# Weights' decoding without a clamp, the normalisation's scaling on ScalarE, and other places for banks, weight sums and scales at the passage to the second network

## Chip, cores and metric

The kernel runs on one core of one Trainium2 chip. The metric is the device time of one execution in microseconds (us); the time of the kernel before is the median of three runs. One further execution was profiled, and all rows below are of that one. The core has a matrix engine (TensorE, PE in the rows; its weight loads are PEld), and VectorE (DVE), ScalarE (ACT), GpSimd (POOL) and SyncE (SP), which here only issues transfers. Each of them works through its own queue in order. Matmuls write into PSUM, which has eight banks of 128 x 512 words.

## Reference

Three stages follow each other: an attention through 32 packed vectors per head, a first network with a softmax-weighted activation and a normalisation (moe), and a second network with a maximum over three products (moe2).

```python
p_packed = sm_attn(p, k, v)                    # 8 images, 8 heads, 576 x 64
x = sm_attn(q, p_packed, p_packed)             # laid out as 4608 x 512
h = x @ w_in                                   # 4608 x 1024
solu = h * softmax(h)
ln = (solu - mean(solu)) / sqrt(var(solu) + 1e-06) * g_ln
y = ln @ w_out                                 # 4608 x 512
h2 = maximum(maximum(y @ w1, y @ w2), y @ w3)  # 4608 x 768
out = h2 @ w_out2                              # 4608 x 512
```

The weights come as 64-bit floating point numbers, and the kernel turns them into 32-bit ones itself. `sums`, `squares` and `powers` hold one number per token and tile, from which the factor `z` of each token's row is worked out; it is applied when the rows of the result are stored.

## The kernel before

The **first phase** covers attention and moe in 36 tiles of 128 tokens. For each tile `tok_hidden` makes h on TensorE (two PSUM banks of `ps_h`, one buffer), the row maximum on VectorE (L506), the exponential on ScalarE (L508), the product with h on VectorE (L510), the negative mean `nmu` (L512), the squares on ScalarE (L513), two small operations on a power of two (L517, L521), and the scaled row u = (u + nmu) * pw on VectorE (L524). The rows of four tiles are transposed on TensorE (L557), split into a high and a low part by ScalarE (`lh`, L563) and VectorE (`ll`, L564), and multiplied by the weights into y (L575): sixteen steps, eight for each half of the output columns. Each half has two banks, `y0` and `y1` of `ps_y`, which are copied out as `yt` by ScalarE (L242) and VectorE (L244) and stored to `ydram`.

An image's attention is prepared by `Packed` in steps that fill gaps between tiles. `values` scales the packed result into `ppz` (L379, two operations of VectorE), TensorE transposes it (L383) and VectorE copies it out as `ppT` (L244). `product` then multiplies `ppT` by `w_in_sb` (L395).

**Decoding.** `decode` turns a piece of 64-bit weights in `raw` into 32-bit ones: ScalarE takes the high word's absolute value into `dt` (L116), VectorE clamps it (L121), shifts and masks it (L122), puts the sign back (L125), isolates the power (L128) and multiplies the low word by it, into `dt` again (L130); GpSimd adds both parts (L135). `dt` of the later pieces has one buffer. Eight pieces of 512 columns for `w_in` and four for `w_out` are followed by 56 of 256 columns for the rest of `w_out` and for moe2, whose results go to `wdram` and `wodram`. The letter strings in `CFG` place these steps in the tiles: each `D` finishes one piece and begins the next, `A` issues its start early, `T` a transposition, `y` a step of y, `F` a step of an image's preparation.

**The passage.** After the last tile the steps of the last y group alternate with the list `before`: sums and splits of y for moe2 (`sums_y`, L680; `splits_y`, L695 and L696), and the weight sums of moe2's first cell (`split_w`: splits L623 and L624, sums L630). Then come the operations of `scales` on VectorE (L531 to L549) and **moe2** in 54 cells, each of seven products into four banks m0 to m3 (L719), added up on VectorE as `u` (L754), `v` (L758), `kept`, `cur` and `r`. The weight sums of cell n + 1 are chores of cell n.

A scheduler orders all of this: it takes instructions in the order of the code, as priorities, and places each engine's queue by its own estimates and by the buffers that are free. The order on an engine can so differ from that of the code.

Of the kernel before, what the change touches and what calls it, by code (L numbers as in the profile page):

```python
# [8 lines left out]
F32 = mybir.dt.float32  # L9
# [9 lines left out]
def f32(ap):  # L19
# [8 lines left out]
    ppT='v',  # L28
    pTz='s',
    yt='sv',  # L30
    ln='v',
# [18 lines left out]
    pz='v',  # L50
# [4 lines left out]
def kernel(  # L55
# [50 lines left out]
    def decode(dst, raw, t, t2=None, add=nc.gpsimd):  # L106
# [5 lines left out]

        lo, hi = raw[:, :, 0], raw[:, :, 1]

        def start():
            nc.scalar.activation(t, f32(hi), AF.Abs)  # L116
            if t2 is not None:
                nc.scalar.activation(t2, lo.bitcast(U32), AF.Copy, scale=2.0 ** -52)

        def rest():  # L120
            nc.vector.tensor_scalar_max(t, t, 2.0 ** -15)  # L121
            nc.vector.tensor_scalar(  # L122
                t.bitcast(I32), t.bitcast(I32), 3, 0x3FFFFFF8, op0=ALU.logical_shift_left, op1=ALU.bitwise_and
            )
            nc.vector.scalar_tensor_tensor(  # L125
                out=hi, in0=hi, scalar=-0x40000000, in1=t.bitcast(I32), op0=ALU.bitwise_and, op1=ALU.bitwise_or
            )
            nc.vector.tensor_scalar(t.bitcast(I32), hi, -0x800000, None, op0=ALU.bitwise_and)  # L128
            if t2 is None:
                nc.vector.scalar_tensor_tensor(  # L130
                    out=t, in0=lo.bitcast(U32), scalar=2.0 ** -52, in1=t, op0=ALU.mult, op1=ALU.mult
                )
            else:
                nc.gpsimd.tensor_tensor(out=t, in0=t2, in1=t, op=ALU.mult)
            add.tensor_tensor(out=dst, in0=f32(hi), in1=t, op=ALU.add)  # L135
# [134 lines left out]
    class Packed:  # L270
# [91 lines left out]
        def values(self, g):  # L362
# [12 lines left out]
            for r in range(2):  # L375
                if CFG['pz'] == 's':
# [7 lines left out]
            ev('ppT', ppT[b][:, g, :], tp[:, :P])  # L384
# [104 lines left out]
    def tok_hidden(t):  # L489
# [34 lines left out]
        nc.vector.tensor_scalar(u, u, nmu, pw, op0=ALU.add, op1=ALU.mult)  # L524
        lnt[t] = u

    def scales():


        vv, z, w = (z_p.tile([P, NT // P], F32, name=n) for n in ("vv", "z", "w"))  # L530
        nc.vector.tensor_scalar_add(sums, sums, 1e-9)  # L531
        nc.vector.tensor_mul(vv, sums, sums)
        nc.vector.tensor_scalar_mul(vv, vv, 1e-6)
        nc.vector.scalar_tensor_tensor(
            out=vv, in0=squares, scalar=1.0 / DFF, in1=vv, op0=ALU.mult, op1=ALU.add
        )
        nc.vector.tensor_scalar(z.bitcast(I32), vv.bitcast(I32), 1, None, op0=ALU.logical_shift_right)
        nc.vector.tensor_scalar(
            z.bitcast(I32), z.bitcast(I32), -1.0, float(0x5F3759DF), op0=ALU.mult, op1=ALU.add
        )  # L540
        for _ in range(3):
# [4 lines left out]
        nc.vector.tensor_scalar(  # L546
# [385 lines left out]
    for _ in range(2 * KFF):  # L932
        step_y(j, 2 * KFF)
        step_t(j, done[j] + CFG['look'])
        if before:
            before.pop(0)()
# [116 lines left out]
```

## Time and profile before

| | us |
|---|---|
| three runs, median | 1150.48 |
| three runs, lowest and highest | 1149.1, 1150.9 |
| the profiled execution | 1150.95 |
| its span, first to last instruction | 1149.2 |
| TensorE busy in the span | 1073.6 (93%) |
| VectorE busy | 775.7 (68%) |
| ScalarE busy | 442.9 (39%) |
| GpSimd busy | 290.9 (25%) |

A busy share over the whole span mixes stages with different limits, so the stages are read one by one: the beginning (0 to 61), the first tiles (61 to 102), the tiles 4 to 22 with decoding beside them (102 to 388), the tiles after the decoding (388 to 533), the passage (533 to 640) and moe2. A busy TensorE is not TensorE at its peak, since the ends of matmuls are modelled. The granted clock is given as a share of 2.4 GHz.

### The profile page before, as it was taken

To read this page: it belongs to the slowest core of one execution; us is meant where nothing else is said; L and a number is where in the kernel's file an instruction comes from. 1 tells how busy PE (TensorE), PEld (TensorE's weight loads), DVE (VectorE), ACT (ScalarE), POOL (GpSimd) and SP (SyncE) were. 2 spreads that over 40 slices of the span, in tenths; PEclk is the share of its full clock that TensorE was granted. 3 is DMA by queue.
4 is the path that set the end of the run, shared out by engine and by line. 5 is a ranking of instruction groups with operands and counts; after the bars stand their busy time and mean duration, and the time that the engine had idled before them with its cause. 6 is when DMAs were issued, how large, how long until landed. Compare 5 with 4: busy or idle time off the path is not lost.

```text
span 1149.2 us, 17628 instructions
## 1 busy us (share of the span) xinstructions
PE 1073.6 (93%) x6308; PEld 890.0 (77%) x6308; DVE 775.7 (68%) x1528; ACT 442.9 (39%) x909; POOL 290.9 (25%) x283
## 2 busy tenths in 40 slices
PE   4689999899898999999787999999999999999998
PEld 2356667576675777687686989989999999998996
DVE  6899897988979685775586754574583573572561
ACT  4467465555554545444333331142132132133012
POOL 4552221121212100000657340041041131032002
PEclk9899999999999999999888999999999999999999
DMA  9753536555454513210464444453453353342421
GB/s 254 166 124 87 144 104 182 146 155 144 133 162 126 150 50 81 70 60 37 147 216 145 154 145 138 133 170 116 123 178 115 120 165 120 123 143 82 137 84 55
DMA packets 132263, 149.01 MB, mean 130 GB/s; under 512 B 51536, under 2 KB 85328, under 8 KB 132176
## 3 DMA queue, kind: packets, MB, share of 16 engines
q1 hardware_dynamic: 132176, 147.89, 43.1%
q8 instruction: 50, 0.82, 0.3%
q14 instruction: 37, 0.30, 0.1%
HBM read 113.25 MB, written 34.60 MB: 129 GB/s over the span
## 4 chain that ended last, share of the span: by engine, by line
PE 62%; DVE 16%; issue 10%; POOL 5%; ACT 3%; DMA 3%; SPq 0%; POOLq 0%; DVEq 0%; ACTq 0%
PE m L719 30%; PE o L956 13%; PE y L575 7%; PE h L500 4%; POOL wt L135 2%; PE mp L395 2%; PE tp L557 2%; DVE raw L125 2%; POOL s L624 1%; DVE dt L128 1%; PE tp L412 1%; DVE dt L121 1%; ACT dt L116 1%; DVE u L510 1%; DVE dt L122 1%
## 5 line engine op out<-in xcount | busy, mean ns | idle before, releaser
L575 PE MATMUL y<-ll,woh 128*128 128x512 f32 x288 | 116.5, 405 | 5.5 <-DVE ll L564 5.4
L754 DVE TENSOR_TENSOR u<-m,q 128x384 f32<-128x384 f32 x54 | 29.9, 553 | 135.9 <-ACT ob L965 75.4
L575 PE MATMUL y<-lh,woh 128*128 128x512 f32 x288 | 117.4, 416 | 3.6 <-ACT yt L242 2.7
L575 PE MATMUL y<-lh,wol 128*128 128x512 f32 x288 | 115.3, 400 | 0.0
L781 POOL TENSOR_TENSOR hl<-cur,hh 128x384 fp32r<-128x384 f32 x36 | 37.9, 1052 | 243.3 <-ACT hh L780 243.2
L135 POOL TENSOR_TENSOR wt<-raw,dt 128x256 f32<-128x256 f32 (+1 forms) x60 | 49.9, 831 | 194.5 <-DVE dt L130 97.4
L750 ACT COPY q<-m 128x384 f32<-128x384 f32 x54 | 25.9, 479 | 171.7 <-PE m L719 171.7
L956 PE MATMUL o<-w2h,hh 128*128 128x512 f32 x216 | 85.8, 397 | 0.0
L956 PE MATMUL o<-w2h,hl 128*128 128x512 f32 x216 | 85.8, 397 | 0.0
L956 PE MATMUL o<-w2l,hh 128*128 128x512 f32 x216 | 85.7, 397 | 0.0
L575 PEld LDWEIGHTS y<-ll,woh 128*128 128x128 f32 x288 | 54.8, 190 | 20.0 <-DVE ll L564 7.8
L719 PE MATMUL m<-b22h,s 128*128 128x384 f32 x216 | 65.8, 345 | 3.1 <-DVE r L741 2.0
L575 PEld LDWEIGHTS y<-lh,woh 128*128 128x128 f32 x288 | 54.2, 189 | 18.3 <-ACT yt L242 3.3
L719 PE MATMUL m<-t1h,s 128*128 128x384 f32 x216 | 63.8, 335 | 2.6 <-DVE r L741 2.6
L575 PEld LDWEIGHTS y<-lh,wol 128*128 128x128 f32 x288 | 54.9, 191 | 12.9 <-issue 0.5
L719 PE MATMUL m<-t2h,s 128*128 128x384 f32 x216 | 64.2, 337 | 0.0
L719 PE MATMUL m<-t3h,s 128*128 128x384 f32 x216 | 63.5, 334 | 0.0
L563 ACT ACTIVATE lh<-tp,g_sb 128x512 fp32r<-128x512 f32 x72 | 47.2, 684 | 31.7 <-PE tp L557 31.5
L781 POOL TENSOR_TENSOR hl<-kept,hh 128x384 fp32r<-128x384 f32 x36 | 38.6, 1071 | 72.6 <-ACT hh L780 72.6
L742 DVE TENSOR_TENSOR kept<-r,kept 128x384 f32<-128x384 f32 x72 | 55.0, 764 | 2.0
L506 DVE TENSOR_REDUCE nm<-h 128x1 f32<-128x1024 f32 x36 | 43.9, 1220 | 16.7 <-PE h L500 16.5
L564 DVE SCALAR_TENSOR_TENSOR ll<-tp,g_sb,lh 128x512 fp32r<-128x512 f32 x72 | 52.0, 740 | 4.0 <-ACT lh L563 3.9
(185 smaller groups left out, 2892.8 us busy)
## 6 DMA issues: line engine op xcount, KB each, us to landing
s<-sdram SPq DMA_DIRECT2D x180, 256.0 KB, 2.8
kt<-in_k_dram SPq DMA_DIRECT2D x16, 576.0 KB, 5.3
vt<-in_v_dram SPq DMA_DIRECT2D x16, 576.0 KB, 4.7
ydram<-yt SPq DMA_DIRECT2D x36, 256.0 KB, 2.8
raw<-in_moe_w_dram SPq DMA_DIRECT2D x36, 256.0 KB, 2.8
b<-ydram SPq DMA_DIRECT2D x24, 384.0 KB, 3.4
sdram<-s SPq DMA_DIRECT2D x36, 256.0 KB, 2.1
out_dram<-ob SPq DMA_DIRECT2D x36, 256.0 KB, 2.0
```

What stands on the lines that cost most here:

```text
L135: add.tensor_tensor(out=dst, in0=f32(hi), in1=t, op=ALU.add)
L500: nc.tensor.matmul(h[:, n, :], lhsT=x, rhs=m[:, g, n * 512:(n + 1) * 512], start=(i == 0), stop=(i == len(ops) - 1),)
L506: nc.vector.tensor_reduce(out=nm, in_=hv, axis=AX.X, op=ALU.max, negate=True)
L563: nc.scalar.activation(lh, tp, AF.Copy, scale=gc)
L564: nc.vector.scalar_tensor_tensor(out=ll, in0=tp, scalar=gc, in1=f32(lh), op0=ALU.mult, op1=ALU.subtract)
L575: nc.tensor.matmul(ys[half][m], lhsT=w[:, kc, ms], rhs=x, start=(kc == 0 and i == 0), stop=(kc == KFF - 1 and i == 2),)
L719: nc.tensor.matmul(out, lhsT=w, rhs=y, start=start and i == 0, stop=i == len(ops) - 1, skip_group_check=not start,)
L742: add(out=cur[m, n], in0=r, in1=cur[m, n], op=ALU.max)
L750: nc.scalar.copy(q, ba)
L754: add(out=u, in0=bb, in1=q, op=ALU.add)
L781: nc.gpsimd.tensor_tensor(out=hl, in0=t, in1=f32(hh), op=ALU.subtract)
L956: nc.tensor.matmul(ops[i], lhsT=x[:, ts], rhs=w, start=(c == 0 and n == 0), stop=(c == KF2 - 1 and n == 2),)
```

## The change

1. **Decoding.** ScalarE now copies the high word with a factor (Copy instead of Abs), and the clamp is gone: four operations of VectorE remain where five were. The mask and the sign constant are wider. In pieces without a second temporary the product goes into the low word's place in `raw`, and GpSimd's addition reads both parts from `raw`, so that `dt` is read by VectorE alone.
2. **The normalised row.** VectorE multiplies the two numbers per token (`nmu` * `pw`, 128 x 1), and ScalarE makes u = u * pw + nmu over 1024 columns (L525 of the kernel after).
3. **Image 0.** Its `ppz` and `ppT` are made by ScalarE.
4. **Fewer decoding steps a tile.** From tile 8 on a tile has two `D` instead of three.
5. **The passage.** The last group's second half of y goes into the two banks of `ps_h` instead of those of the first half. Weight sums stand behind VectorE's and ScalarE's last `ll` and `lh` (`issue_after`), and those of the second cell are made here too. `scales` becomes chores of the cells 2 to 7. `ps_o` is laid out ahead of `ps_m`.

```diff
 def decode(dst, raw, t, t2=None, add=nc.gpsimd):
-            nc.scalar.activation(t, f32(hi), AF.Abs)
+            nc.scalar.activation(t, f32(hi), AF.Copy, scale=2.0 ** -112)
...
-            nc.vector.tensor_scalar_max(t, t, 2.0 ** -15)
             nc.vector.tensor_scalar(
-                t.bitcast(I32), t.bitcast(I32), 3, 0x3FFFFFF8, ...
+                t.bitcast(I32), t.bitcast(I32), 3, 0x7FFFFFF8, ...
...
-                    out=t, in0=lo.bitcast(U32), scalar=2.0 ** -52, in1=t, ...
+                    out=f32(lo), in0=lo.bitcast(U32), scalar=2.0 ** -52, in1=t, ...
+                add.tensor_tensor(out=dst, in0=f32(hi), in1=f32(lo), op=ALU.add)
...
-        nc.vector.tensor_scalar(u, u, nmu, pw, op0=ALU.add, op1=ALU.mult)
+        nc.vector.tensor_mul(nmu, nmu, pw)
+        nc.scalar.activation(u, u, AF.Identity, bias=nmu, scale=pw)
...
+    s2='DFNTAHTTyTyDyTAFy',
-                if CFG['pz'] == 's':
+                if b == 0:
                     nc.scalar.activation(ppz[:, r, :], pv[:, :D], AF.Copy, scale=...)
-            ev('ppT', ppT[b][:, g, :], tp[:, :P])
+            ev('ppT', ppT[b][:, g, :], tp[:, :P], min(b, 1))
...
+            if j == NB - 1 and half:
+                h = ps_h.tile([P, 2, 512], F32, tag="h", name="y")
+                ys[half] = [h[:, m, :] for m in range(KDM // 2)]
...
-    before = [*sums_y(0), *splits_y(0), *w_steps]
+    w_steps2 = split_w(0, 1, w0_p)
+    w_steps2.pop(0)()
+    before = [*sums_y(0), *splits_y(0), w_steps[5]]
+    behind = [w_steps[6], *w_steps[1:5], *w_steps2[:5]]
...
+        if n >= KFF and behind:
+            with tc.issue_after(last[nc.vector].ins), tc.issue_after(last[nc.scalar].ins):
+                behind.pop(0)()
+                if behind and n % 2:
+                    behind.pop(0)()
...
+    ps_o = ctx.enter_context(tc.tile_pool(name="ps_o", bufs=4, ...))
     ps_m = ctx.enter_context(tc.tile_pool(name="ps_m", bufs=1, ...))
-    ps_o = ctx.enter_context(tc.tile_pool(name="ps_o", bufs=4, ...))
...
+    for i, f in enumerate(scales(z)):
+        chores.setdefault(2 + i, []).append(f)
```

The scheduler places the queues anew. At three places they read as follows.

VectorE at the beginning, image 0's second group of heads: `ri` and `rim` are the reciprocal sums by which `ppz` is scaled, `dt` and `raw` belong to decoding. Before:

```order
L346 TENSOR_SCALAR ri_332<-se_329 128x1
L125 SCALAR_TENSOR_TENSOR raw<-raw,dt 128x512
L121 TENSOR_SCALAR dt<-dt 128x512
L128 TENSOR_SCALAR dt<-raw 128x512
L122 TENSOR_SCALAR dt<-dt 128x512
L130 SCALAR_TENSOR_TENSOR dt<-raw,dt 128x512
L125 SCALAR_TENSOR_TENSOR raw<-raw,dt 128x512
L347 RECIPROCAL ri_332<-ri_332 128x1
L128 TENSOR_SCALAR dt<-raw 128x512
L349 TENSOR_SCALAR rim<-par,ri_332 128x2
L379 TENSOR_SCALAR ppz<-pv,rim 128x64 x2
```

and after:

```order
L337 TENSOR_SCALAR m_316<-m_316 128x1
L346 TENSOR_SCALAR ri_324<-se_321 128x1
L347 RECIPROCAL ri_324<-ri_324 128x1
L349 TENSOR_SCALAR rim<-par,ri_324 128x2
L121 TENSOR_SCALAR dt<-dt 128x512
```

The three operations that lead to `rim` now stand together, and the two of `ppz` are in ScalarE's queue.

ScalarE in a tile of the middle (`u` and `h` are the tile's row and PSUM banks, `qT` an image's queries). Before:

```order
L508 ACTIVATE u,sums<-h,nm 128x1024
L513 ACTIVATE h,squares<-u,nmu 128x1024
L116 ACTIVATE dt<-raw 128x256
L242 COPY qT<-tp 128x384
L242 COPY qT<-tp 128x192
L242 COPY yt<-y_2947 128x512
```

and after:

```order
L508 ACTIVATE u,sums<-h,nm 128x1024
L116 ACTIVATE dt<-raw 128x256
L513 ACTIVATE h,squares<-u,nmu 128x1024
L242 COPY qT<-tp 128x384
L242 COPY qT<-tp 128x192
L116 ACTIVATE dt<-raw 128x256
L525 ACTIVATE u<-u,nmu,powers 128x1024
```

The added operation stands some places behind the squares, and copies that TensorE waits for stand behind it.

VectorE at the passage, where the last `ll` of the last y group are made (`s` are weight sums, `b22l` is a split of y). Before:

```order
L564 SCALAR_TENSOR_TENSOR ll<-tp,g_sb,lh 128x512 x2
L696 TENSOR_TENSOR b22l<-b_5969,b22h 128x768
L564 SCALAR_TENSOR_TENSOR ll<-tp,g_sb,lh 128x512
L630 TENSOR_TENSOR s_6165<-wt_5961,s_6141 128x256
L630 TENSOR_TENSOR s_6302<-wt_6237 128x256
L630 TENSOR_TENSOR s_6304<-s_6302,wt_6235 128x256
L564 SCALAR_TENSOR_TENSOR ll<-tp,g_sb,lh 128x512
L630 TENSOR_TENSOR s_6317<-wt_6235,wt_6237 128x256
```

and after:

```order
L573 SCALAR_TENSOR_TENSOR ll<-tp,g_sb,lh 128x512 x2
L714 TENSOR_TENSOR b22l<-b_5937,b22h 128x768
L573 SCALAR_TENSOR_TENSOR ll<-tp,g_sb,lh 128x512 x2
L646 TENSOR_TENSOR s_6092<-wt_5931 128x256
L646 TENSOR_TENSOR s_6106<-wt_5929,wt_5931 128x256
```

All eight `ll` now stand ahead of the weight sums. The operations of `scales` still stand between the last weight sums and moe2's first `u`, in both kernels.

## Rows read from the trace of the kernel before

**Rows 1.** Stages: us, busy us of each engine (instructions), clock, DMA share, GB/s

```profile
0.00:61.00 61.00, 37.17 (x266) 21.07 (x267) 44.74 (x86) 27.95 (x64) 28.67 (x32) 0.89 0.81 210
61.00:102.00 41.00, 36.48 (x297) 22.69 (x296) 38.06 (x83) 28.54 (x62) 16.64 (x16) 1.00 0.37 97
102.00:388.00 286.00, 265.77 (x1761) 190.35 (x1760) 245.88 (x632) 157.04 (x352) 63.26 (x80) 0.98 0.51 143
388.00:506.00 118.00, 117.27 (x805) 86.93 (x804) 84.22 (x173) 58.40 (x117) 6.82 (x7) 1.00 0.28 80
...
533.00:640.00 107.00, 88.32 (x413) 76.75 (x412) 74.46 (x119) 42.05 (x88) 63.86 (x61) 0.90 0.48 155
640.00:1149.20 509.20, 501.59 (x2652) 470.57 (x2651) 272.56 (x411) 118.48 (x209) 111.64 (x89) 1.00 0.40 127
```

**Rows 2.** L524 alone by stage, one a tile: VectorE's busy us (count), clock, DMA

```profile
61.00:102.00 41.00, 3.23 (x4) 1.00 0.37 97
102.00:388.00 286.00, 18.57 (x19) 0.98 0.51 143
388.00:506.00 118.00, 8.27 (x9) 1.00 0.28 80
506.00:533.00 27.00, 2.44 (x3) 1.00 0.05 20
```

**Rows 3.** VectorE's groups by line, 102 to 388: count, busy us, mean ns, idle before

```profile
L125 DVE SCALAR_TENSOR_TENSOR raw<-raw,dt 128x256 int32<-128x256 int32 x56 | 24.5, 437 | 0.9
L130 DVE SCALAR_TENSOR_TENSOR dt<-raw,dt 128x256 f32<-128x256 uint32 x56 | 23.3, 416 | 0.5
L128 DVE TENSOR_SCALAR dt<-raw 128x256 int32<-128x256 int32 x56 | 17.7, 316 | 0.7
L122 DVE TENSOR_SCALAR dt<-dt 128x256 int32<-128x256 int32 x56 | 17.5, 313 | 0.5
L121 DVE TENSOR_SCALAR dt<-dt 128x256 f32<-128x256 f32 x56 | 17.5, 312 | 19.8 <-ACT dt L116 19.5
...
L521 DVE TENSOR_SCALAR powers<-powers 128x1 int32<-128x1 int32 x19 | 2.8, 148 | 0.2
```

**Rows 4.** ScalarE's groups by line, 102 to 388

```profile
L116 ACT ACTIVATE dt<-raw 128x256 f32<-128x256 f32 x55 | 23.9, 434 | 47.7 <-POOL wt L135 43.0 <-DMA raw<-in_moe_w_dram 3.9 <-DMA raw<-in_moe_w_out_dram 0.5
L513 ACT ACTIVATE h<-u,nmu 128x1024 f32<-128x1024 f32 x19 | 21.3, 1123 | 15.5 <-DVE nmu L512 15.5
```

**Rows 5.** TensorE's waits, 0 to 61: us in total, times, longest

```profile
PE tp L383 <- DVE ppz L379: 11.6, 2, 6.0
```

**Rows 6.** VectorE in order of time, 28 to 39: start, duration

```profile
30.07 0.20 DVE L346 TENSOR_SCALAR ri<-se 128x1 f32<-128x1 f32 x1
...
31.78 1.49 DVE L121 TENSOR_SCALAR dt<-dt 128x512 f32<-128x512 f32 x1
...
36.16 0.15 DVE L347 RECIPROCAL ri<-ri 128x1 f32<-128x1 f32 x1
...
37.59 0.22 DVE L349 TENSOR_SCALAR rim<-par,ri 128x2 f32<-128x2 f32 x1
```

**Rows 7.** TensorE's waits, 533 to 640

```profile
PE m L719 <- DVE v L758: 6.3, 3, 3.4
PE y L575 <- DVE ll L564: 3.6, 3, 2.9
PE y L575 <- ACT yt L242: 2.7, 1, 2.7
```

**Rows 8.** Two stretches of the passage, columns as in rows 1

```profile
558.60:565.40 6.80, 4.12 (x11) 2.83 (x10) 4.26 (x5) 2.35 (x7) 5.38 (x7) 0.50 0.61 211
582.50:589.30 6.80, 5.81 (x18) 5.81 (x19) 5.74 (x19) 2.01 (x5) 3.32 (x4) 0.50 0.58 174
```

**Rows 9.** VectorE in order of time at moe2's first cell

```profile
575.69 1.27 DVE L532 TENSOR_TENSOR vv<-sums 128x36 f32<-128x36 f32 x1
...
580.31 1.20 DVE L542 TENSOR_TENSOR w<-z 128x36 f32<-128x36 f32 x1
...
581.65 0.55 DVE L754 TENSOR_TENSOR u<-m,q 128x384 f32<-128x384 f32 x1
```

More of the change, by code (lines that the diff above doesn't have):

```diff
@@ L523, in tok_hidden, with scales, variance, guess @@
         )
-        nc.vector.tensor_scalar(u, u, nmu, pw, op0=ALU.add, op1=ALU.mult)
+        nc.vector.tensor_mul(nmu, nmu, pw)
+        nc.scalar.activation(u, u, AF.Identity, bias=nmu, scale=pw)
         lnt[t] = u
[L527 to L541, printed above, removed]
+    def scales(z):
+        vv, w = (z_p.tile([P, NT // P], F32, name=n) for n in ("vv", "w"))
+        def variance():
+            nc.vector.tensor_scalar_add(sums, sums, 1e-9)
+            nc.vector.tensor_mul(vv, sums, sums)
+            nc.vector.tensor_scalar_mul(vv, vv, 1e-6)
+            nc.vector.scalar_tensor_tensor(
+                out=vv, in0=squares, scalar=1.0 / DFF, in1=vv, op0=ALU.mult, op1=ALU.add
+            )
+        def guess():
+            nc.vector.tensor_scalar(z.bitcast(I32), vv.bitcast(I32), 1, None, op0=ALU.logical_shift_right)
+            nc.vector.tensor_scalar(
+                z.bitcast(I32), z.bitcast(I32), -1.0, float(0x5F3759DF), op0=ALU.mult, op1=ALU.add
+            )
+        def newton():
             nc.vector.tensor_mul(w, z, z)
@@ L569, in y_product @@
         if kc == 0:
-            ys[half] = [ps_y.tile([P, TB], F32, tag=f"y{m}", name=f"y{m}") for m in range(KDM // 2)]
+            if j == NB - 1 and half:
+                h = ps_h.tile([P, 2, 512], F32, tag="h", name="y")
+                ys[half] = [h[:, m, :] for m in range(KDM // 2)]
+            else:
+                ys[half] = [ps_y.tile([P, TB], F32, tag=f"y{m}", name=f"y{m}") for m in range(KDM // 2)]
         lh, ll = lnT[kc]
@@ L868 @@
         j, i = t // 4 - 1, t % 4
-        for x in CFG['s0'][t] if j < 0 else CFG['s1']:
+        for x in CFG['s0'][t] if j < 0 else CFG['s2' if j else 's1']:
             if x == 'H':
@@ L973 @@
     chores = {}
-    prep = [split_w(*cells[n][1:], wpool if cells[n][1] else w0_p) for n in range(1, NC)]
-    prep[0][0]()
+    prep = [w_steps2] + [split_w(*cells[n][1:], wpool if cells[n][1] else w0_p) for n in range(2, NC)]
+    prep[1][0]()
     for n in range(NC - 1):
-        load_next = prep[n + 1][0] if n + 1 < len(prep) else lambda: None
-        chores[n] = [load_next, lambda: None, *prep[n][1:]]
+        load_next = prep[n + 1][0] if n and n + 1 < len(prep) else lambda: None
+        chores[n] = [load_next, lambda: None, *(prep[n][1:6] if n else ())]
         if n < KF2:
@@ L992, in fresh @@
         return sums_of[p]
-    z = scales()
     kept, first_half, ops = [], [], None
```

44 lines of the change are left out of this document (24 added, 20 removed).

## The prediction

> **What bounds the kernel now.** I read the stages first, one row for each [rows 1]. The reader should look at TensorE's busy time against the length, and at VectorE beside it. From 640 on TensorE is busy 501.6 of 509.2 us and nothing in the change touches that work, so the 509 us stay. From 388 to 506, after the decoding, it is busy 117.3 of 118: TensorE bounds there too, while VectorE works 84.2, which is 71%. From 102 to 388 it is otherwise. VectorE works 245.9 of 286 us (86%), and TensorE, which idles 20.2 us, also gets through its work more slowly than its own pace allows. L524 runs once a tile, so its count gives the tiles [rows 2]: 19 in the long stretch, or 15.05 us each, and 9 in the one behind it, or 13.11 us each. The matmul records of a tile are nearly as many, 1761/19 = 92.7 against 805/9 = 89.4 [rows 1]. At the later pace a tile of the long stretch would take 13.11 x 92.7/89.4 = 13.6 us. The long stretch thus loses 1.4 us a tile to something else, and what it has more of is decoding.
>
> Two more places lose time. In the first 61 us two waits for `ppz` hold TensorE for 11.6 us, the longest 6.0 [rows 5]. In the passage TensorE idles 107 - 88.3 = 18.7 us, and its clock is 0.90 in the mean [rows 1]; the longest waits are for `v`, for `ll` and for `yt` [rows 7].
>
> **The change part by part.** Durations are those of the profiled execution, 1150.95 us with a span of 1149.2, which lies 0.5 us above the median of the three runs.
>
> *Tiles 4 to 22.* The clamp takes 56 x 0.312 = 17.5 us off VectorE [rows 3]. The scaled row takes 18.6 us off [rows 2] and leaves a product of 128 x 1; its nearest row is L521, 0.148 us [rows 3], so 19 x 0.148 = 2.8 comes back and 15.8 is saved. With two `D` a tile, nine of the 56 pieces move behind tile 22, as VectorE's new order shows; at 0.437 + 0.416 + 0.316 + 0.313 = 1.48 us each [rows 3] that is 13.3 us. VectorE keeps 245.9 - 17.5 - 15.8 - 13.3 = 199.3 us. The loop through `dt` opens too: ScalarE waited 43.0 us in all for GpSimd's addition before it could write `dt` again [rows 4], and VectorE 19.5 us for ScalarE behind that [rows 3]. GpSimd no longer reads `dt`, so the wait and all that is queued behind it on ScalarE, copies out of PSUM among them, come free. TensorE's pace is late next: 19 x 13.6 = 258 us, in which VectorE would be busy 77%. I take 286 - 258 = **28 us**. The low end is half of TensorE's idle time, 10 us; the high end is all that leaves VectorE, 46.6 us, as if TensorE had waited for each bit of it.
>
> The price is on ScalarE: 19 operations over 1024 columns, bounded by L513 of the same size, 1.12 us [rows 4], and a wait in front of each for VectorE's three small operations. L513 itself waits 15.5/19 = 0.82 us for VectorE [rows 4]; I take that for the new wait. It comes to 19 x 1.94 = 37 us, and 157 [rows 1] + 37 = 194 of 258 us, 75%. Queued behind it are the next exponential and the copies of `qT`, `kT` and `lh`. I cost it at nothing in this stretch since TensorE's own pace covers it, and price the other case as a rival.
>
> *Tiles 0 to 3.* VectorE is busy 38.1 of 41 us [rows 1], and loses 4 x (0.81 - 0.15) = 2.6 us and two clamps of 512 columns, which lie between the 0.31 of 256 columns and the 1.49 us of the slow one [rows 3, 6]. I take **3 us** (0 to 5).
>
> *Tiles 23 to 35.* Nine pieces arrive, 13.3 us, and 8.27 - 9 x 0.148 = 6.9 leave, so VectorE goes from 84.2 to 90.6 of 118 us. TensorE idled 0.7 us here; at the long stretch's 7% it would idle 8. I take a loss of **2 us** (0 to 8).
>
> *The beginning.* `rim` of the second group waits on VectorE from L346 at 30.07 to L349's end at 37.81, with decoding in between, of which one clamp took 1.49 us [rows 6]. In the new order L346, L347 and L349 stand together, 0.57 us in all, and `ppz` goes to ScalarE, where each half, at 128 x 64, costs no more than L116's 0.43 us at 128 x 256 [rows 4]. So the wait of 6.0 us should go; the other of 5.6 mostly stays, since ScalarE's `ppz` stands behind exponentials that need a maximum from VectorE behind decoding. Late next is GpSimd's addition of the last `w_in` pieces, which moves only by the clamps ahead of it. I take **5 us**, between 1 and all 11.6.
>
> *The passage.* With all eight `ll` ahead of the weight sums the wait of 2.9 us goes, and with idle banks that of 2.7 for `yt` [rows 7]. `v` waits 3.4 us because VectorE does small operations of `scales` from 575.7 until `u` at 581.65, some of 1.2 us [rows 9]. They still stand ahead of `u`, only partly earlier, so I take 2.4 of the 3.4. The clock stood at 0.50 of 2.4 GHz, its lower level, in 558.6 to 565.4 and 582.5 to 589.3, just after or while TensorE waited [rows 8]. It was busy 4.1 and 5.8 us there, so half of that, 4.9 us, is lost, and would come back with the waits gone. One cell's weight sums leave the following cells: 1 us. In all 13.9, taken as **14 us**; the low end, 6, is the two sure waits, the high end, 24, is all idle time and this clock loss. The moved steps bring two weight loads and four stores forward in SP's queue, past two stores of `yt`; GpSimd's added splits fall into TensorE's last eight steps of y. The two pools of banks change places; a wait for that is not in the rows and I cost it at nothing.
>
> The sum is 28 + 3 - 2 + 5 + 14 = 48 us, and 1150.95 - 48 = **1103 us**.
>
> A point on contention. L524 takes 0.98 us where GpSimd is busy 63 us and 2.44/3 = 0.81 where it is silent, between 506 and 533 [rows 1, 2]. Part of the removed duration may thus be waiting for GpSimd. If that part, 19 x 0.16 = 3 us, passed on to the next operation of VectorE and were waited for in full, the time would be 1106. The Trainium skill, "SBUF — State Buffer", section "Who interferes with whom", states that a two-port operation of VectorE and one of GpSimd take a shared port pair in turns and that the loser waits for the whole instruction. By that rule the wait is GpSimd's making and could move so. The rows agree with a rule of that kind, with 0.98 against 0.81 us.
>
> **The rivals.**
>
> *Half of it in the long stretch.* If only 10 of the 28 us come, because TensorE's slow pace there has other reasons (attention's short matmuls, ScalarE's chain), the time is 1121. For it: VectorE is busy 86%, not full. Against it: the pace of the tiles right behind, with the same work but for decoding.
>
> *More than that.* If both waits for `ppz` go (6.6 more), and the tiles of the long stretch run without any loss to VectorE (10 more of the high end), it is 1086. For it: ScalarE and VectorE lose 43.0 and 19.5 us of waiting on top of their work. Against it: TensorE then would have to beat the pace it kept when it was 99% busy.
>
> *The removed wait comes back as GpSimd's.* The 1106 above.
>
> *ScalarE holds the tiles, and the kernel is slower.* One h buffer serves all tiles, and the squares free it. If L525 with its wait, 1.94 us, lay in front of that in each of 36 tiles and nothing covered it, it would add 70 us: 1103 + 70 = 1173. It decides from the point where ScalarE's queue is full; at 75% it is not, and a tile of 13 us would need 48/36 = 1.3 us of each L525 uncovered to lose the whole gain. The Trainium skill, "ScalarE: Activation LUTs", section "Rules for kernel authors", puts additions and multiplications on VectorE rather than ScalarE; by that rule this is the wrong way round. The rows agree that ScalarE takes longer, 1.12 against 0.98 us, but not that it is the engine that is short.
>
> *It does not do what it says.* The scheduler might bring decoding and weight sums back between what TensorE waits for. Its order shows this only for `scales`. Then the beginning and the passage give their low ends and the long stretch nothing: about 1150 - 10 + 8 = 1148, hardly a change.
>
> **How the numbers follow.** Forecast, 1088 to 1118 around 1103: 0.52. Half: 0.17. More: 0.15. GpSimd's wait: 0.08. No change: 0.03. Slower: 0.05. The first four are faster, 0.92. The likeliest gives 1103. From 1080 to 1125 the range takes in the forecast with the bounds of its terms, the rival with more, the rival with half and GpSimd's, and leaves out what lies beyond either. A measurement of this kernel can tell 0.2%, 2.3 us, from no change: faster 0.92, same 0.03, slower 0.05.
>
> **What would show it.** In the profile after, tiles 4 to 22 should take some 258 us with VectorE near 77% and ScalarE near 70 to 75%, and no wait of ScalarE for GpSimd's addition; the decoding should end some four tiles later. L525 should last about 1.12 us with under 1 us of waiting. The wait before the second `ppz` should be under 1 us and `v`'s in the first cell near 1. Waits for `ll` behind weight sums, and for `yt`, should be gone, and the clock should stay at 1.00 from 545 us of the old count to the first cells. I am wrong if TensorE's waits for ScalarE grow by more than 10 us, if the long stretch keeps over 15 us a tile though VectorE is below 80%, or if the gain comes mainly from moe2.

## The result and the profile after

The changed kernel takes 1121.37 us (median of four runs, 1120.28 to 1122.70), beside 1149.79 us for the kernel before on the same chip. The ratio is 0.9754, with a 95% interval of 0.9736 to 0.9773, so 28.4 us are gained. A second group of runs of the unedited changed kernel, further down, gave 1119.52 us and 0.9748. The profiled run is one of 1121.45 us, its span 1119.7.

In the lines of the kernel after, the decoding is L116, L121, L124, L127, L129 and GpSimd's addition L132. The small product is L524 and the scaled row on ScalarE L525. In the passage L632 loads weights, L646 forms a weight sum, L639 and L640 split one on ScalarE and GpSimd, L651 stores the split, L534 to L557 are `scales`, and L768, L772 and L776 are `q`, `u` and `v` of a cell.

First the stages, the counterpart of [rows 1]. Columns: us, then busy us (instructions) of TensorE, its weight load, VectorE, ScalarE and GpSimd, then clock, DMA share and GB/s.

```profile
0.00:58.00 58.00, 34.30 (x265) 20.06 (x266) 37.61 (x70) 29.33 (x70) 23.24 (x32) 0.82 0.86 221
58.00:101.00 43.00, 38.94 (x291) 24.15 (x290) 35.36 (x80) 32.26 (x65) 14.99 (x16) 0.92 0.35 86
101.00:363.00 262.00, 255.82 (x1772) 187.65 (x1765) 213.58 (x542) 174.68 (x364) 48.91 (x71) 1.00 0.53 145
363.00:481.00 118.00, 116.67 (x797) 85.86 (x796) 89.45 (x206) 71.43 (x134) 12.08 (x16) 1.00 0.37 107
...
508.00:610.50 102.50, 87.00 (x420) 75.48 (x419) 74.77 (x122) 42.93 (x89) 62.40 (x61) 0.93 0.49 162
610.50:1119.70 509.20, 501.58 (x2652) 470.54 (x2650) 270.20 (x411) 118.59 (x209) 112.29 (x89) 1.00 0.42 127
```

The long stretch went from 286 to 262 us, the passage from 107 to 102.5, and moe2's 2652 instructions take the same 509.2. Cut exactly, at the starts of VectorE's maximum over h in tiles 0, 4, 23 and 35, the stages of the kernels with undone or added parts are these (us, one profiled run each). The last two columns tell what else differs in a stage: how many of the 56 pieces of 256 columns VectorE decodes in tiles 4 to 22, and for how many us TensorE is busy at a granted clock of 0.50, in tiles 0 to 3 and in tiles 4 to 22.

| kernel | to tile 0 | tiles 0-3 | tiles 4-22 | 23 to start of 35 | from there on | pieces in 4-22 | busy at 0.50, tiles 0-3 / 4-22 |
|---|---|---|---|---|---|---|---|
| before | 61.4 | 40.7 | 286.1 | 144.5 | 616.5 | 56 | 0 / 10.2 |
| after | 58.5 | 42.4 | 262.2 | 145.2 | 611.4 | 47 | 6.8 / 0 |
| after, run again | 58.1 | 39.9 | 261.7 | 145.2 | 611.5 | 47 | 0 / 0 |
| row on VectorE again | 59.9 | 40.5 | 268.6 | 145.1 | 610.1 | 46 | 3.3 / 9.5 |
| clamp alone again | 61.2 | 44.6 | 264.0 | 146.3 | 611.8 | 44 | 10.0 / 0 |
| loop alone closed again | 59.9 | 39.9 | 272.1 | 145.1 | 611.0 | 47 | 0 / 3.4 |
| both (old decoding) | 62.7 | 45.3 | 265.8 | 146.1 | 610.3 | 43 | 13.4 / 0 |
| three pieces a tile again | 57.3 | 42.4 | 274.4 | 143.6 | 611.2 | 56 | 6.8 / 3.4 |
| ppz on VectorE again | 61.1 | 44.7 | 261.1 | 145.2 | 611.1 | 47 | 6.5 / 0 |
| old passage | 57.8 | 42.4 | 262.9 | 145.7 | 617.1 | 47 | 6.8 / 0 |
| scales, sums and y sums late | 58.4 | 39.9 | 263.1 | 145.2 | 608.6 | 47 | 0 / 0 |

Half of the time in the last column is what the lower clock can have cost, an estimate that supposes the same work at 1.00 to take half as long. Two such stretches, of the kernel before and of the one with the row on VectorE again (columns as in the rows above):

```profile
302.60:306.00 3.40, 3.40 (x9) 2.64 (x8) 3.40 (x10) 1.10 (x4) 0.79 (x2) 0.50 0.52 158
165.10:171.90 6.80, 6.05 (x28) 3.01 (x27) 4.94 (x14) 2.52 (x7) 1.54 (x1) 0.50 0.52 148
```

Next the groups of the long stretch in the kernel after, 101 to 363 us, which answer to [rows 3] and [rows 4]: first VectorE's, then ScalarE's. Columns: count, busy us, mean ns, idle before and what ended it.

```profile
L129 DVE SCALAR_TENSOR_TENSOR raw<-raw,dt 128x256 f32<-128x256 uint32 x47 | 20.5, 436 | 1.1
L124 DVE SCALAR_TENSOR_TENSOR raw<-raw,dt 128x256 int32<-128x256 int32 x47 | 19.7, 419 | 2.2
L121 DVE TENSOR_SCALAR dt<-dt 128x256 int32<-128x256 int32 x47 | 16.1, 342 | 19.6 <-ACT dt L116 19.5
L127 DVE TENSOR_SCALAR dt<-raw 128x256 int32<-128x256 int32 x47 | 14.5, 308 | 1.0
...
L524 DVE TENSOR_TENSOR nmu<-nmu,powers 128x1 f32<-128x1 f32 x19 | 4.8, 251 | 0.3
```

```profile
L525 ACT ACTIVATE u<-u,nmu,powers 128x1024 f32<-128x1024 f32 x19 | 23.6, 1242 | 1.4 <-DVE nmu L524 1.0
L513 ACT ACTIVATE h<-u,nmu 128x1024 f32<-128x1024 f32 x19 | 21.3, 1120 | 17.8 <-DVE nmu L512 17.8
```

Nine pieces of 56 have left, as forecast. L525 is dearer than L513, 1.24 against 1.12 us, but it hardly waits: 1.4/19 = 0.07 us each. VectorE still waits 19.5 us for ScalarE's `dt`, exactly as before.

The passage, 508 to 640, is the counterpart of [rows 7]: TensorE's waits, us in total, times, longest.

```profile
PE m L737 <- DVE v L776: 9.7, 5, 5.1
PE m L737 <- DVE cur L785: 2.5, 2, 1.6
PE m L737 <- ACT q L768: 1.6, 2, 1.4
```

The waits for `ll` and `yt` are gone. The longest one, for `v` in the first cell, grew from 3.4 to 5.1 us. VectorE in order of time shows why (start, duration, and in brackets idle before):

```profile
546.13 0.43 DVE L646 TENSOR_TENSOR s<-wt 128x256 f32<-128x256 f32 x1 [5.12 <-DMA wt<-wdram]
546.48 0.42 DVE L646 TENSOR_TENSOR s<-wt,wt 128x256 f32<-128x256 f32 x1
546.81 0.96 DVE L646 TENSOR_TENSOR s<-s,wt 128x256 f32<-128x256 f32 x1
547.70 0.18 DVE L535 TENSOR_TENSOR vv<-sums 128x36 f32<-128x36 f32 x1
...
551.73 1.17 DVE L550 TENSOR_SCALAR w<-w 128x36 f32<-128x36 f32 x1
552.82 0.54 DVE L772 TENSOR_TENSOR u<-m,q 128x384 f32<-128x384 f32 x1
...
554.06 0.99 DVE L646 TENSOR_TENSOR s<-wt,s 128x256 f32<-128x256 f32 x1
554.97 0.55 DVE L776 TENSOR_TENSOR v<-m,u 128x384 f32<-128x384 f32 x1
```

VectorE stands idle for 5.12 us because the third cell's weights are late, and only then come three weight sums, then `scales`, then `u`. SP's queue in order of time tells why the weights are late:

```profile
537.13 5.48 SPq L651 DMA_DIRECT2D sdram<-s  x6
542.67 1.58 SPq L632 DMA_DIRECT2D wt<-wdram  x3
```

Six stores of splits, each of which waits for GpSimd, stand ahead of the second of the third cell's two loads. They come late themselves: the first load had held SP's queue from 515.0 to 532.0 us, until VectorE's weight sums, which now stand behind the last `ll`, had read the buffer that it fills (SP's waits, 520 to 560):

```profile
SPq L632 <- DVE s L646: 18.1, 3, 17.0
```

### The profile page after: what moved, and what is told of

Read it like the earlier page. It is cut to its first block, busy times and chain, and to the rows that moved or that the text cites. A ratio compares the mean times of both kernels' runs of the same rounds, so it can differ in the third digit from the quotient of the medians.

```text
span 1119.7 us, 17559 instructions
## 1 busy us (share of the span) xinstructions
PE 1061.3 (95%) x6308; PEld 885.5 (79%) x6308; DVE 735.0 (66%) x1454; ACT 483.9 (43%) x951; POOL 273.9 (24%) x283
## 4 chain that ended last, share of the span: by engine, by line
PE 52%; DVE 4%; issue 3%; POOL 2%; ACT 1%; DMA 1%; SPq 0%; DVEq 0%; POOLq 0%; ACTq 0%
PE m L737 31%; PE o L984 13%; PE y L591 4%; PE h L500 2%; POOL s L640 1%; PE tp L566 1%; DMA wt<-wdram 1%; DVE s L646 1%; DVE v L776 0%; POOL al L640 0%; DVE u L772 0%; PE mp L395 0%; DVE u L510 0%; DVE nm L506 0%; DVE r L759 0%
## 5 line engine op out<-in xcount | busy, mean ns | idle before, releaser
L772 DVE TENSOR_TENSOR u<-m,q 128x384 f32<-128x384 f32 x54 | 29.9, 554 | 134.7 <-ACT ob L993 75.7
L768 ACT COPY q<-m 128x384 f32<-128x384 f32 x54 | 25.9, 480 | 168.2 <-PE m L737 168.2
L132 POOL TENSOR_TENSOR wt<-raw 128x256 f32<-128x256 f32 x56 | 34.4, 615 | 213.3 <-DVE raw L129 116.9
L798 ACT CAST hh<-cur 128x384 fp32r<-128x384 f32 x36 | 18.5, 514 | 90.4 <-DVE cur L785 49.0
L506 DVE TENSOR_REDUCE nm<-h 128x1 f32<-128x1024 f32 x36 | 43.9, 1219 | 17.8 <-PE h L500 17.5
```

Of the source, the lines that this page charges most:

```text
L132: add.tensor_tensor(out=dst, in0=f32(hi), in1=f32(lo), op=ALU.add)
L506: nc.vector.tensor_reduce(out=nm, in_=hv, axis=AX.X, op=ALU.max, negate=True)
L768: nc.scalar.copy(q, ba)
L772: add(out=u, in0=bb, in1=q, op=ALU.add)
L798: nc.scalar.copy(hh, t)
```

## Experiments

Each ratio is to the kernel before, measured beside it on the same chip; "a cost of" compares with 0.9751, the mean of the changed kernel's two ratios, at 11.5 us for each 0.01. The intervals are some 0.002 to 0.003 to either side, so a cost is known to some 3 us. The stages are those of a single run each, which can lie above its kernel's median: by 4.1 us with the old decoding, 1.8 with the row on VectorE, 1.6 with three pieces, 1.4 with `ppz` on VectorE and 2.1 with scales and sums late.

### The long stretch: four parts undone, one at a time

The scaled row back on VectorE:

```diff
-        nc.vector.tensor_mul(nmu, nmu, pw)
-        nc.scalar.activation(u, u, AF.Identity, bias=nmu, scale=pw)
+        nc.vector.tensor_scalar(u, u, nmu, pw, op0=ALU.add, op1=ALU.mult)
```

> Only the scaled row goes back: the operation over 128 x 1024 is VectorE's again, as before, in all 36 tiles; everything else stays as in the changed kernel. Theory A, VectorE's time: in the stretch of tiles 4 to 22 the change took some 46.6 us of work off VectorE and the stretch became 23.9 us shorter, that is 0.51 us for each us. Putting 19 x (0.98 - 0.15) = 15.8 us back costs 8.1 us there, and 2 to 3 us more in tiles 0 to 3, where VectorE was nearly full: 1131 us. Rival, ScalarE pays: the row on ScalarE takes 1.24 us and stands in front of the next exponential and copies; if that eats what VectorE gains, the time stays at 1121 us (1119 to 1123), or falls below it.

Measured: 1124.22 us, ratio 0.9783 (0.9758 to 0.9809), a cost of 3.7 us. That is theory A's direction and a third of its 10 us; it lies outside the 1119 to 1123 of the rival, by which ScalarE eats what VectorE gains. The long stretch became 6.4 us longer (8.1 expected) and the last stage 1.3 us shorter. But TensorE was busy 9.5 us of that stretch at a clock of 0.50, where the changed kernel has none of it, so up to 4.7 of the 6.4 us can be the clock's, and one profile does not tell whether the edit brought that about.

Three pieces a tile again:

```diff
-    s2='DFNTAHTTyTyDyTAFy',
+    s2='DFNTAHTDTyATyDyTAFy',
```

> Only the number of pieces goes back: three D a tile from tile 8 on (the table of the later tiles is that of the first ones again), new decoding. Theory A, VectorE's time: nine pieces of 1.5 us come back into the long stretch, 13.3 us at 0.51, or 6.8 us, and leave the tiles behind, which gives 0.7 back: 1127 us. Rival C, the number of pieces does not matter once the clamp and the row are gone: 1121 us (1119 to 1123).

Measured: 1129.08 us, 0.9814 (0.9782 to 0.9847), a cost of 7.2 us: as theory A has it in total. By stages it is 12.2 us in the long stretch, of which up to 1.7 can be the clock's, and 1.6 back behind it.

The whole old decoding, with clamp and closed loop:

```diff
-            nc.scalar.activation(t, f32(hi), AF.Copy, scale=2.0 ** -112)
+            nc.scalar.activation(t, f32(hi), AF.Abs)
...
+            nc.vector.tensor_scalar_max(t, t, 2.0 ** -15)
...
-                    out=f32(lo), in0=lo.bitcast(U32), scalar=2.0 ** -52, in1=t, op0=ALU.mult, op1=ALU.mult
+                    out=t, in0=lo.bitcast(U32), scalar=2.0 ** -52, in1=t, op0=ALU.mult, op1=ALU.mult
...
-                add.tensor_tensor(out=dst, in0=f32(hi), in1=f32(lo), op=ALU.add)
+                add.tensor_tensor(out=dst, in0=f32(hi), in1=t, op=ALU.add)
```

> Only the decoding goes back: with clamp, the product written into dt, and GpSimd's addition reading dt, so that the loop through dt is closed again; two D a tile and all else stay as in the changed kernel. Theory A, VectorE's time: some 47 clamps of 0.312 us in the long stretch, 14.7 us at 0.51, are 7.5 us, and 1 to 2 us in the first 100 us: 1130 us. Rival B, the loop: ScalarE's 43 us of waiting for GpSimd and what was queued behind it were the larger part of the gain: 1137 us or more.

Measured: 1127.91 us, 0.9821 (0.9792 to 0.9850), a cost of 8.0 us. The total is near theory A's, but not the place: only 3.6 us of it lie in the long stretch, and 7 to 10 in the stages before it (against the changed kernel's two profiles), of which up to 3.3 and 6.7 can be the clock's in tiles 0 to 3. Clamp and loop had to be told apart. First the loop alone, by the last four changed lines of that diff without the others:

> The decoding has no clamp, as in the changed kernel, but the product goes into dt again and GpSimd's addition reads dt, so that ScalarE's next write of dt waits for GpSimd. VectorE's work is the same. Theory A, VectorE's time: 1121 us (1119 to 1123), though ScalarE will show some 40 us of waiting for GpSimd. Rival B, the loop: ScalarE's waits hold its copies out of PSUM and VectorE behind them, and the time is 8 us or more higher, 1129 us or more.

Measured: 1130.77 us, 0.9842 (0.9816 to 0.9868), a cost of 10.5 us, 9.9 of it in the long stretch (up to 1.7 of that the clock's). Rival B holds: VectorE's work is the same and the time is not. The group of ScalarE's first decoding step in that stretch shows the wait:

```profile
L116 ACT ACTIVATE dt<-raw 128x256 f32<-128x256 f32 x47 | 20.5, 436 | 25.1 <-POOL wt L132 19.7 <-DMA raw<-in_moe_w_dram 3.4 <-DMA raw<-in_moe_w_out_dram 2.0
```

Then the clamp alone, by the first lines of the diff (absolute value, clamp and old masks), with the loop open:

> The clamp goes back alone: the decoding has the absolute value, the clamp and the old masks, but its product is still written over the low words, so that GpSimd does not read dt and the loop stays open. Theory A, VectorE's time: 47 clamps of 0.312 us in the long stretch are 14.7 us, at 0.51 that is 7.5 us, and 1 to 2 us come in the first 100 us: 1128 to 1130 us. Rival B, the loop: what the old decoding cost (7.7 us) and what the closed loop without clamp cost (10 us) is the loop's alone, and the clamp is covered: 1120 to 1123 us.

Measured: 1129.63 us, 0.9819 (0.9792 to 0.9846), a cost of 7.8 us. The sum that theory A gives is met, but again not where it said: 1.8 us in the long stretch, 1.1 behind it, and some 5 to 8 us in the first 106 us, where `w_in` is decoded in pieces of 512 columns; of these up to 1.6 (of the 5) and 5.0 (of the 8) can be the clock's in tiles 0 to 3. So the two halves of the decoding each cost 8 to 10 us when undone alone, and 8 when undone together: they are not additive.

In the long stretch a closed loop with the clamp takes 265.8 us, without it 272.1, although the clamp is one operation more for each piece. The stretches do not hold the same pieces. One group of VectorE's in it, one operation a piece, first with loop and clamp and then with the loop alone:

```profile
L125 DVE SCALAR_TENSOR_TENSOR raw<-raw,dt 128x256 int32<-128x256 int32 x43 | 19.1, 444 | 0.8
L124 DVE SCALAR_TENSOR_TENSOR raw<-raw,dt 128x256 int32<-128x256 int32 x47 | 19.7, 419 | 0.7
```

With the clamp decoding runs later, and four more pieces fall behind tile 22, where TensorE is the bound. By the run with three pieces a piece in the stretch is worth 12.2/9 = 1.36 us, or 1.2 without the clock's part, so four are about 5 us; with the clock's up to 1.7 us in the loop's stretch this is as much as the 6.3. At equal pieces, as an estimate, clamp and loop together cost some 9 us in the stretch, the loop alone 10 and the clamp alone (44 pieces) 6.

### The beginning

```diff
-                if b == 0:
+                if False:
                     nc.scalar.activation(ppz[:, r, :], pv[:, :D], AF.Copy, scale=self.rim[g][:, r:r + 1])
```

with `ppT` on VectorE throughout, as before.

> Only the first image's ppz (four scalings of 128 x 64) and its ppT copies go back to VectorE. Theory A: the move is worth what the two waits show, 11.6 us in the kernel before against 8.9 in the changed one, and the shorter time to tile 0: 2 to 4 us, 1124 us. Rival B: the second wait only moved into the first, which became 7.7 instead of 5.6 us, and what comes after is set by decoding: 1121 us (1119 to 1122).

Measured: 1123.55 us, 0.9780 (0.9762 to 0.9799), a cost of 3.3 us. That is theory A's number, but its reason does not hold. Of the kernel after, and then of this one, TensorE's wait in the first 58 us:

```profile
PE tp L383 <- ACT ppz L377: 8.9, 2, 7.7
```

```profile
PE tp L383 <- DVE ppz L379: 7.6, 2, 5.6
```

With `ppz` on VectorE the two waits are shorter in sum, and their second transposition starts at the same time. The eight products behind it do not take the same; TensorE in order of time, in the kernel after and then in this one:

```profile
35.84 0.33 PE L383 MATMUL tp<-ident,ppz 128*128 128x128 f32 x1 [1.11 <-ACT ppz L377]
36.09 1.94 PE L395 MATMUL mp<-w_in_sb,ppT 128*64 128x512 f32 x8
```

```profile
35.67 0.44 PE L383 MATMUL tp<-ident,ppz 128*128 128x128 f32 x1 [1.98 <-DVE ppz L379]
36.05 3.68 PE L395 MATMUL mp<-w_in_sb,ppT 128*64 128x512 f32 x8
```

In the kernel before these eight took 3.68 us too, at a clock of 0.50; here the records of the clock begin only at 40.8 us. So 1.7 of the 2.6 us by which tile 0 is later lie in these products, likely by TensorE's clock, and none in the two waits; what ScalarE's `ppz` is worth by itself stays open.

Between the kernel before and the one after, the second wait fell from 6.0 [rows 5] to 1.1 us, but the first one rose from 5.6 to 7.7 (6.3 in the second profile of the changed kernel). With `ppz` on VectorE the second is 2.0 us, so most of its fall does not need ScalarE. On ScalarE the `ppz` of group 0 stands behind group 1's exponentials, which wait for VectorE:

```profile
28.49 0.50 ACT L341 ACTIVATE e<-s,m 128x288 f32<-128x288 f32 x1 [7.32 <-DVE m L337]
...
29.46 0.52 ACT L377 ACTIVATE ppz<-pv,rim 128x64 f32<-128x64 f32 x2
```

### The passage

All its edits undone: weight sums one a step among the last y products, the second cell's in the first cell, `scales` ahead of the cells, y's last half in its own banks, the pools in the old order.

> Only the passage goes back: weight sums of the first cell one a step among the last y products, those of the second cell in the first cell, scales ahead of the cells, y's last half in its own banks and the two bank pools in their former order. Theory A: the stages of the profile give the passage its true worth, 616.5 - 611.4 = 5.1 us, and the rest of the 14 forecast was lost to the longer wait for v: 1126 to 1127 us, with v's wait back at about 3.4 us and the waits for ll and yt back. Rival B: the passage's edits gained nothing and the 5.1 us are clock and chance: 1121 us. Rival C: they gained the 14 us forecast and something of the new first phase takes 9 back behind tile 35: 1135 us.

Measured: 1126.74 us, 0.9806 (0.9787 to 0.9825), a cost of 6.3 us; the last stage is 617.1 us, 5.7 more, and the first four agree with the changed kernel's within 0.7 us each. `v`'s longest wait is 3.4 us again, and those for `ll` (3.6 in all) and `yt` (2.2) are back (TensorE's waits, 508 to 640):

```profile
PE m L737 <- DVE v L776: 5.9, 4, 3.4
PE y L591 <- DVE ll L573: 3.6, 3, 2.9
...
PE y L591 <- ACT yt L242: 2.2, 1, 2.2
```

Theory A holds: the passage's edits are worth what the stage shows, not the 14 us forecast.

`scales` bound behind the sixth cell's `u`:

```diff
+    def pinned(f):
+        with tc.issue_after(last[nc.vector].ins):
+            f()
...
-        chores.setdefault(2 + i, []).append(f)
+        chores.setdefault(5 + i // 3, []).append(lambda f=f: pinned(f))
```

(where `last` holds the latest `u`).

> The small operations of scales are bound behind VectorE's u of moe2's sixth cell; nothing else moves. Theory A: they are what stands between the weight sums and u in the first cell, and v's wait falls from 5.1 to 1 us or less: 1117 us. Rival B, the load: VectorE stands idle until 546 us for the weights of the third cell, whose sums are ahead of u too, so that most of the wait stays even without scales: v's wait 3 us or more and 1120 to 1121 us.

Measured: 1121.25 us, 0.9758 (0.9737 to 0.9779): no gain. VectorE in order of time, in this kernel:

```profile
546.13 0.42 DVE L646 TENSOR_TENSOR s<-wt 128x256 f32<-128x256 f32 x1 [4.92 <-DMA wt<-wdram]
...
549.13 0.56 DVE L772 TENSOR_TENSOR u<-m,q 128x384 f32<-128x384 f32 x1 [0.77 <-ACT q L768]
551.67 1.47 DVE L646 TENSOR_TENSOR s<-wt,s 128x256 f32<-128x256 f32 x1 [1.98 <-POOL s L640]
553.06 0.55 DVE L776 TENSOR_TENSOR v<-m,u 128x384 f32<-128x384 f32 x1
```

`u` came 3.7 us earlier and `v` only 1.9. Between them stands the third cell's fourth weight sum, which waits for GpSimd to read the buffer that it overwrites. The wait for `v` fell to 3.2 us, so the numbers are rival B's, by a reason that was only half named: the sums as such, not only their late load.

The same, and the third cell's weight sums bound behind the first cell's `u`:

```diff
+    chores[1] = [chores[1][0]] + [lambda f=f: behind_u(f) for f in chores[1][1:7]] + chores[1][7:]
+
+    def behind_u(f):
+        with tc.issue_after(last['u0'].ins):
+            f()
```

> As in the run with late scales, and the weight sums of the third cell are bound behind u of the first cell, so that the late load of its weights holds up neither u nor v. Theory A, scales alone: no better than with late scales only, 1117 us. Rival B, the load: this one gains the 4 to 5 us, 1116 to 1117, where late scales alone gain none. A new wait is possible in the third cell, whose sums come later: if the sums are then last, it loses 1 to 3 us there.

Measured: 1117.66 us, 0.9722 (0.9699 to 0.9745). In the first cell `v`'s wait is 1.5 us and the ratio has moved as rival B has it. But the profile does not show the gain in its place: the last stage is 611.3 us, as in the changed kernel. TensorE's waits, 506 to 640:

```profile
PE m L737 <- DVE v L777: 9.7, 6, 2.4
PE m L737 <- ACT q L768: 2.5, 2, 1.6
```

The 5.1 us are spread over six waits with the same sum of 9.7. What is shorter in this profile, with a span of 1118.0 us, is tiles 0 to 3, 39.9 us, which the changed kernel has too when its clock stays up (below). So by the stage something behind the first cell bounds it; whether the 3 us of the ratio are the edit's is not settled by this run. Between 566 and 586 us VectorE is busy 19.30 of 20 us in the kernel after, and four differences of y for the second half of the tokens (L698, 0.94 to 1.57 us each) stand there among the first cells' results. Bound behind the first result of their own, later cells:

```diff
-            chores.setdefault(NC * p - 5 + i, []).append(lambda p=p, i=i: fresh(p)[i]())
+            chores.setdefault(NC * p - 5 + i, []).append(lambda p=p, i=i: pinned(fresh(p)[i]))
```

> As with scales and the third cell's sums late, and the four differences of y for the second half of the tokens, and scales, are bound behind the first result of their own cell, so that they no longer stand in the first four cells. Theory A, VectorE is the bound of the first cells (9 to 10 of 10 us busy between 566 and 586): taking 4 operations of 0.9 to 1.6 us out of that stretch, some 4.5 us, shortens the waits for v, cur and kept after the first cell, 2 to 4 us: 1114 to 1117 us, and the last stage below 610. Rival B, GpSimd's splits are the bound: VectorE only waits for them instead, and the time is that of the run before, 1117 to 1119 us, with the last stage at 611.

with the unedited kernel beside it:

> The changed kernel once more, unedited, as the yardstick for the two runs beside it: 1121 us (1119 to 1123), v's wait in the first cell about 5 us, and in the stage from the last tile to the end some 611.4 us. By every theory no difference.

and with the first image's `ppz` shared (`if b == 0 and g == 1` for ScalarE):

> As the run beside it, and the first image's ppz is shared: group 0 on VectorE, group 1 on ScalarE. Theory A: ScalarE's ppz of group 0 stands behind the exponentials of group 1, which wait for VectorE; on VectorE it comes earlier, the first wait falls from 7.7 to 5.6 us or less and the second stays at 1.1: 2 us less than the run beside it. Rival B: the following work is bound to the same decoding and takes the 2 us back: no difference.

Measured: the changed kernel 1119.52 us, 0.9748 (0.9726 to 0.9769); y sums late 1116.23 us, 0.9720 (0.9699 to 0.9742); with `ppz` shared 1115.92 us, 0.9713 (0.9693 to 0.9734). The runs of the changed kernel lie between 1118.19 and 1120.90, those with late y sums between 1115.12 and 1118.06; the gain of 3.3 us is seen, although the intervals of the ratios overlap. The last stage is 608.6 us with the y sums late and 608.3 with `ppz` shared too, 2.9 and 3.2 less than with the unedited kernel beside them, which is theory A's mark. Against the run with the sums alone the ratio is no better (0.9720 and 0.9722), so how the 3 us divide between the two edits rests on the stages alone. In the same 20 us of two kernels, first after and then with the y sums late:

```profile
566.00:586.00 20.00, 15.45 (x83) 13.91 (x82) 19.30 (x29) 7.44 (x17) 13.85 (x14) 1.00 0.74 239
```

```profile
566.00:586.00 20.00, 15.05 (x79) 13.26 (x78) 14.45 (x22) 7.25 (x17) 15.05 (x16) 1.00 0.70 229
```

VectorE is no longer full, and TensorE's waits in 506 to 640 are 7.5 us for `v` in place of 9.7. This kernel is faster than the changed one and the one before. Sharing `ppz` leaves waits of 5.2 and 0.6 us in the first 58 us instead of 7.0 to 8.9 in all, and brings tile 0 forward by 0.4 us: within what two profiles of one program differ by (58.1 and 58.5), so rival B stands there.

## Why the prediction was right or wrong

The direction and the main place were right: most of the gain, 23.9 us of the stages' 29.5, lies in tiles 4 to 22, where VectorE was relieved. The time came out 18 us above the forecast, at the number of the rival "half of it", but not for its reason: the long stretch gave 24 of its 28 us, not 10. That this rival's number was met is chance. By stages the missing 18.5 us are 8.9 in the passage, 4.7 in tiles 0 to 3, 4.1 in the long stretch and 2.1 in the beginning, less 1.3 in tiles 23 to 35.

*Tiles 4 to 22, forecast 28, measured 23.9.* The forecast was TensorE's pace of the tiles behind, 258 us, and TensorE is busy 255.8 us in the stretch; but it still idles 6.2 us (20.2 before). The step "VectorE keeps 245.9 - 17.5 - 15.8 - 13.3 = 199.3 us" failed: it keeps 213.6, or 82% instead of 77%. Most of the removed work did go. Summed by their own durations, VectorE's instructions in the stretch fell from 284.3 to 241.2 us, 43.1 less, where 46.6 were forecast; the small product took 0.251 us in place of 0.148, which is 2.0 us of the rest. But the busy time of [rows 1] counts overlapping instructions once, and it fell by 32.3. Each instruction's record overlaps the next: 0.43 us begun at 546.13 is followed by one at 546.48. I took durations off a busy time in which they were not fully contained.

Part of the 23.9 is not VectorE's for sure. The old stretch had TensorE busy 10.2 us at a clock of 0.50, the new one none, which is up to 5.1 us. I had put the whole 1.4 us a tile down to decoding, although [rows 1] give a clock of 0.98 there; whether the removed waits or chance took those drops away is not shown.

Of the three parts, by undoing: pieces 12.2 us, row 6.4, old decoding 3.6, in sum 22.2 of the 23.9; by share of durations I would have had 8.0, 9.5 and 10.5. These are no clean prices: up to 4.7 of the row's and 1.7 of the pieces' can be the clock's, and the old decoding has four pieces fewer in its stretch, about 5 us. So no order among the three is shown.

*The price on ScalarE.* L525 was bounded by L513's 1.12 us and took 1.24, and the wait I put ahead of it, 0.82, was 0.07: ScalarE gets there later than VectorE's product. ScalarE is at 67% and not 75% chiefly for another reason: my 194 us counted 15.6 us of waiting as work and left in the first step of the nine pieces that went, 3.9 us. That nothing queued behind it would cost the gain held: the slower rival, 1173 us, has no support. The Trainium skill, "ScalarE: Activation LUTs", section "Rules for kernel authors", gives additions and multiplications to VectorE; the run with the row there was 3.7 us slower, so the measurement decides against it here, where VectorE is the fuller engine.

*The loop through `dt`.* The wait of ScalarE for GpSimd is gone, as forecast; the 19.5 us of VectorE behind ScalarE, which I counted to the same loop, are still there. With the new decoding a closed loop costs 10.5 us.

*Tiles 0 to 3, forecast 3, measured -1.7 in the profile shown, 0.8 in the second.* The two are the same program. In the first TensorE's clock was at 0.50 from 91.4 to 98.2 us, while TensorE was busy all of it; in the second it stayed at 1.00.

```profile
91.40:98.20 6.80, 6.80 (x23) 4.48 (x23) 5.47 (x13) 3.09 (x5) 1.55 (x1) 0.50 0.22 66
```

That half clock can cost up to 3.4 us and covers the difference of 2.5. The forecast of 3 was too high even without it. The old kernel had no such drop there, and I had not priced one.

*The beginning, forecast 5, measured 2.9 to 3.3.* "The wait of 6.0 us should go; the other of 5.6 mostly stays": the first half held (1.1), the second did not (7.7), for the reason that I named myself, ScalarE's exponentials ahead of `ppz`, and then costed at nothing. The fall of the 6.0 is only partly ScalarE's doing: with `ppz` on VectorE and the rest of the change in place it is 2.0.

*Tiles 23 to 35, forecast -2, measured -0.7.* Of VectorE's rise to 90.6 us, 89.45 came, and TensorE hides it.

*The passage, forecast 14, measured 5.1.* The sure part held: the waits for `ll` and `yt`, 5.6 us together in the forecast, went. Two steps failed. "They still stand ahead of `u`, only partly earlier, so I take 2.4 of the 3.4": the wait grew by 1.7 instead. I named the moved loads and stores in SP's queue and gave them no price; a load that waits for VectorE's weight sums and six stores that wait for GpSimd stood ahead of a weight load, and VectorE idled 5.12 us for it with `scales` queued behind. And the clock: "half of that, 4.9 us, is lost, and would come back with the waits gone", but TensorE's waits in this stage went only from 19.4 to 16.2 us, since 9.7 for `v` stand where 6.6 did, and the time in which it is busy at 0.50 from 15.7 to 10.0 us, worth 2.8 at most (each over 131 us from the start of tile 35). Under both lies what neither step looked at: in the first cells VectorE is full (19.30 of 20 us) with sums for later cells, so that clearing one place only makes the next one late. With `scales` bound late, then the weight sums too, then the y sums too, the stage shows this in turn: 612.4, 611.3 and 608.6 us. It does not follow the clock: TensorE is busy at 0.50 for 10.0 us in the changed kernel and 6.6 with scales and sums late, at 611.4 and 611.3 us, and for 3.4 and 10.1 us in the two with the y sums late, at 608.6 and 608.3.

*Contention.* The reading of L524's 0.98 and 0.81 us as GpSimd's doing was weak: it took 0.81 us also from 61 to 102, where GpSimd was busy 16.6 of 41 us, and 0.92 from 388 to 506, where it was busy 6.8 of 118 [rows 1, 2]. In the rival "It does not do what it says" the low ends add up to 7 us, not 10.

By parts undone the sum is 3.7 (row) + 8.0 (decoding) + 7.2 (pieces) + 3.3 (`ppz`) + 6.3 (passage) = 28.5 us, which is the whole gain; that it closes so well is luck, with some 3 us on each and parts that are not additive.

## What to carry to other kernels

When you take instructions off an engine, subtract what its busy time will lose (the distance from one start to the next), not the sum of their durations, and undo each part by itself before crediting it. When you compare a stage of two kernels, first count the work that lies in it and its time at the lower clock: here four pieces that had slipped into the next stage made more work look faster. When you move a step, price its DMA in the queue that it joins: what stands ahead of it there may wait for yet another engine. When a long wait is removed and the sum of waits stays the same, look for the engine that is full over the whole stretch, and take off it what is not due yet.

## What the runs showed of the hardware

In the kernel after, VectorE's operations differ by where their inputs lie. Those that read one input from PSUM take the same with GpSimd busy or not: `u` 549 ns in the mean between 545 and 610 us, where GpSimd is busy beside nearly all of each, and 555 ns between 650 and 1110, where it is silent beside all but three. Those with both inputs in SBUF don't: of the weight sums of 128 x 256 between 500 and 640 us, the nine with GpSimd silent took 0.41 to 0.42 us and the eight with GpSimd busy throughout 0.68 to 1.51. The Trainium skill, "SBUF — State Buffer", section "Who interferes with whom", says that an operation of VectorE with two SBUF inputs contends with GpSimd's reads, and that one with at most one SBUF input, outside the modes that use both port pairs, does not; these rows agree.

TensorE's clock came out differently in executions of the same instructions. Six of the profiles have the same instructions in the same order up to tile 23. In three of them (after, old passage, scales late) TensorE has 6.8 us at 0.50 in tiles 0 to 3, which take 42.4 us; in the other three (after again, scales and sums late, y sums late) it has none, and they take 39.9. Comparing two kernels by a single profile's stage can therefore mislead by 2 to 3 us. For the first stage no such comparison is possible: the records of the clock begin 19.7 us into one profile of the changed kernel and 33.8 us into the other.
